# A chunked recurrence with routed experts: the state read on four TensorE tiles, merged copies, and shared PSUM banks

## The chip, the cores and the metric

One core of one Trainium2 chip. The metric is device time in microseconds (us); the kernel before takes 406.6 us (median of three runs).

## What is computed

First an RWKV recurrence over 4 batches, 8 heads, 768 steps and head size 48, then a top-1 routed mixture of 8 experts on its 3072 rows of 384 numbers, all in fp32:

```python
for t in range(S):
    cur = np.einsum('bhd,bhe->bhde', u[None] * kt, vt)
    y[:, :, t] = np.einsum('bhd,bhde->bhe', rt, state + cur)
    state = wt[:, :, :, None] * state + np.einsum('bhd,bhe->bhde', kt, vt)
...
x = y as rows of 8 * 48 numbers
logits = x @ w_gate
e = argmax(logits); gate_w = softmax(logits)[e]
out = gate_w * (maximum(x @ w1[e], 0) @ w2[e])
```

## The kernel before

The sequence is cut into six chunks of 128 steps. A *block* n = 0..23 is one chunk (n // 4) of one batch (n % 4). The 8 heads of a block are kept as 4 pairs q; the two heads j = 0, 1 of a pair lie on partitions 0 to 47 and 64 to 111 of one tile, so that a pair has 112 rows (RP). Where a matmul contracts over one head it uses half of TensorE's rows (0 to 63 or 64 to 127).

For a block, DVE makes the products of the decays in both directions by scans (`suf`, `pre`) and from them `kh` and `rh`. PE multiplies these to the 128x128 attention blocks of all heads (`ap`, `pe_a`). `at` is prepared as a diagonal (the u term, by ACT from `ct`; two of eight by POOL, `pool_diag`), and DVE copies `ap` into it under the causal mask (`dve_at`, L384, two COPY_PREDICATED of 128x512, one for each j). Into `yp` PE first reads the state of the earlier chunks (`pe_inter`, L493, from n = 4 on: 16 trace instructions per block, since each fp32 matmul is two) and then adds `at` times v (`pe_av`, L515). ACT copies `yp` to `yt` (`act_y`); PE transposes it (`yq`), ACT writes it to the rows `xr` (`act_xr`). For the state, `kh` is transposed (`kp`, ACT copies it to `kt`), multiplied with v (`dp`, `pe_state`, L506), and added by DVE to the decayed state (`sst`, `dve_state`); ACT then decays that into `gbd` (`act_g`). The u term is `cp`, ACT's copy `cs`, PE's `cpt`, ACT's copy `ct`.

The order on PE, DVE, ACT and POOL is written by hand: `iteration(n)`, called for n = -3..23, issues the steps of several blocks in turn (`ap`, state read, `at` and `av` of block n; `suf`, `kh`, `pre`, `rh` and `cp` of block n + 2; the diagonal and `kt` of block n + 1; `yq` and `sst` of block n - 1). Each engine works its own list in this order, and waits in it for data or for a buffer.

Routing runs beside the recurrence. When a chunk is done, `logit_mm` (L529, four column tiles of 32, copied by ACT to `ls`) makes the logits of its four blocks; for two chunks at a time (`whole`, at n = 8 and n = 16) `logit_tr` (L540, tile `lpt`) transposes them and `gate` (L544 ff, DVE) finds the expert; one iteration later `rank` and `place` give each row its place in its expert's list, and POOL scatters the rows to DRAM. The last chunks go in smaller lots (n = 21, 22, 23), block 22 by `pe_logits` (L621 ff, eight-column matmuls into `lg`). From n = 22 on the first expert's matmuls (L292) are mixed in; from about 165 us on the experts alone run, their order made by a scheduler; their PE work is the same whatever the recurrence did.

PSUM has eight banks. Before: `psA` one (half of `ap`), `psX` three in turn for all small results (`cp`, `cpt`, `kp`, `yq`, `lp`, `lpt`, `rank`, `lg` and later ones), `psD` one (`dp`), `psY` one (`yp`), `psT` a two-bank tile shared in turn by `pre(n + 2)` and the other half of `ap(n + 1)`: `ap(n + 1)` can start only when `rh(n + 2)` has been read from it.

Of the kernel before, what the change touches and what calls it, by code (L numbers as in the profile page):

```python
# [46 lines left out]

@with_exitstack
def rwkv_moe_kernel(ctx, tc, rkw, vv, ub, wgp, wg, w1, w2, out):
# [247 lines left out]
    def contract(wt, hs, q, rows, t, o=None):  # L297
        op = psX.tile([rows, DM], F32, name="opt", tag="tp")
# [174 lines left out]
    def pe_a(n):  # L473
        if real(n):
            d = blk[n]
            d["ap"] = [psT.tile([P, 2, BANK], F32, name="ap", tag="t")[:, 1, :].rearrange("p (q c) -> p q c", c=C),
                       psA.tile([P, NP_, C], F32, name="ap", tag="ap")]
            for q in range(NP_):
                for j in range(2):
                    rs = slice(64 * j, 64 * j + (64 if j == 0 else D))  # L480
                    nc.tensor.matmul(d["ap"][j][:, q, :], d["kh"][rs, q, :], d["rh"][rs, q, :], start=True, stop=True)  # L481

    def pe_inter(n):
        if real(n):
            d = blk[n]
            yp = psY.tile([RP, NP_, C], F32, name="yp", tag="yp")
            d["yp"] = yp
            if n >= B:
                for q in range(NP_):
# [19 lines left out]
    def pe_av(n):  # L509
        if real(n):  # L510
            d = blk[n]
            for q in range(NP_):
                for j in range(2):
                    h = 2 * q + j
                    nc.tensor.matmul(d["yp"][64 * j:64 * j + D, q, :], d["v"][:, h * D:(h + 1) * D], d["at"][:, j, q, :],  # L515
                                     start=(n < B and q == 0), stop=(q == NP_ - 1), skip_group_check=True)

    def pe_y(n):
        if real(n):
            yq = psX.tile([P, NP_ * P], F32, name="yq", tag="tp")  # L520
# [69 lines left out]
    def rank(k):  # L590
# [635 lines left out]
```

## Time and profile before

| | |
|---|---|
| three timed runs | 406.78, 406.60, 405.75 us |
| profiled execution | 408.01 us, span 406.3 us |
| mean granted TensorE clock | 0.993 |
| PE busy | 386.5 us (95% of the span) |
| DVE busy | 269.8 us (66%) |
| ACT busy | 234.8 us (58%) |
| POOL busy | 117.8 us (29%) |

The table averages two different programs. Up to about 155 us the recurrence keeps three engines busy at once, and an engine's list is read row by row on the timeline, where a bracket gives idle time and what ended it. After that PE works nearly without a gap.

### The profile page before, as it was taken

How to read it: one execution, taken by the hardware profiler on the slowest of the kernel's cores; microseconds unless marked ns; L12 is line 12 of the kernel's file. 1: busy time of each engine (PE TensorE's matmuls, PEld its weight loads, DVE VectorE, ACT ScalarE, POOL GpSimd, SP SyncE). 2: the span in 40 equal slices, each digit the busy share in tenths (PEclk: the TensorE clock that was granted, in tenths of full speed). 3: DMA queues.
4: the chain of work that ended last, by engine and by line, in shares of the span. 5: the costliest groups of instructions: out<-in, count | busy, mean ns of one | idle time of the engine just before them, and what ended most of it. 6: DMA issues, size and time to landing. Idle time of an engine off the chain costs nothing.

```text
span 406.3 us, 9456 instructions
## 1 busy us (share of the span) xinstructions
PE 386.5 (95%) x3537; PEld 347.6 (86%) x3537; DVE 269.8 (66%) x517; ACT 234.8 (58%) x650; POOL 117.8 (29%) x162
## 2 busy tenths in 40 slices
PE   8798999899999889999999999999999999999994
PEld 6566887777777678989888999999999999999993
DVE  8999899999999885726856562472562672632311
ACT  8989898989989873216754543543552562420200
POOL 6552322685417925210300050040040040221001
PEclk9999999999999998999999999999999999999998
DMA  8999999988741223196688447246246253011001
GB/s 209 217 234 227 244 233 240 248 241 212 193 106 60 80 71 118 47 318 199 201 277 234 150 123 229 90 140 214 81 139 215 77 142 132 11 45 37 18 16 41
DMA packets 30158, 62.04 MB, mean 153 GB/s; under 512 B 4879, under 2 KB 17978, under 8 KB 30108
## 3 DMA queue, kind: packets, MB, share of 16 engines
q1 hardware_dynamic: 25500, 51.92, 47.5%
q0 software_dynamic: 4608, 9.48, 7.0%
q8 instruction: 29, 0.48, 0.5%
q14 instruction: 21, 0.17, 0.1%
HBM read 49.53 MB, written 12.20 MB: 152 GB/s over the span
## 4 chain that ended last, share of the span: by engine, by line
PE 71%; DVE 11%; ACT 11%; issue 3%; DMA 2%; POOL 0%; POOLq 0%; SPq 0%; ACTq 0%; DVEq 0%
PE bank L292 26%; PE bank L943 17%; PE opt L304 10%; ACT at L354 3%; DVE pre L376 3%; PE ap L481 2%; DVE suf L360 2%; PE yp L515 2%; PE pt L283 2%; PE yp L493 2%; ACT gbd L413 2%; PE op L932 2%; PE cpt L463 2%; ACT junk L399 2%; PE dp L506 1%
## 5 line engine op out<-in xcount | busy, mean ns | idle before, releaser
L254 POOL DMA_INDIRECT out_dram<-ot,xg x26 | 29.2, 1124 | 169.8 <-DVE ot L933 127.3
L230 DVE TENSOR_TENSOR w2l<-wst,w2h 128x512 fp32r<-128x512 f32 x48 | 31.2, 684 | 43.6 <-ACT w2h L228 43.6
L292 PE MATMUL bank<-xl,w1h 128*128 128x384 f32 (+5 forms) x168 | 59.1, 353 | 0.0
L292 PE MATMUL bank<-xh,w1l 128*128 128x384 f32 (+5 forms) x168 | 58.7, 350 | 0.0
L292 PE MATMUL bank<-xh,w1h 128*128 128x384 f32 (+5 forms) x168 | 53.7, 351 | 0.0
L294 ACT ACTIVATE hh<-bank 128x384 fp32r<-128x384 f32 (+7 forms) x58 | 26.5, 471 | 38.8 <-PE bank L292 37.2
L354 ACT ACTIVATE at<-ident,ct 128x128 f32<-128x128 f32 x144 | 44.6, 392 | 0.1
L295 DVE SCALAR_TENSOR_TENSOR hl<-bank,hh 128x384 fp32r<-128x384 f32 (+7 forms) x58 | 29.9, 531 | 19.7 <-ACT hh L294 18.4
L327 POOL TENSOR_TENSOR rk<-rkwt 112x512 f32<-112x512 f32 x24 | 31.9, 1328 | 33.7 <-DVE pre L364 30.1
L384 DVE COPY_PREDICATED at<-cmask,ap 128x512 f32<-128x512 int32 x48 | 32.5, 729 | 6.4 <-PE ap L481 4.5
L230 DVE TENSOR_TENSOR w1l<-wst,w1h 128x512 fp32r<-128x512 f32 x48 | 31.5, 684 | 6.4 <-ACT w1h L228 6.4
L948 ACT ACTIVATE oT<-bank 128x464 f32<-128x464 f32 (+4 forms) x15 | 7.9, 524 | 46.0 <-PE bank L943 46.0
L228 ACT ACTIVATE w1h<-wst 128x512 fp32r<-128x512 f32 x48 | 28.6, 628 | 9.9 <-PE bank L292 6.7
L943 PE MATMUL bank<-hh,w2l 128*128 128x408 f32 (+4 forms) x96 | 33.9, 355 | 0.0
L943 PE MATMUL bank<-hl,w2h 128*128 128x408 f32 (+4 forms) x96 | 33.8, 354 | 0.0
L943 PE MATMUL bank<-hh,w2h 128*128 128x408 f32 (+4 forms) x96 | 33.5, 354 | 0.0
L676 POOL DMA_INDIRECT xs<-xr,pi x24 | 28.2, 1174 | 16.7 <-DVE sh L550 4.9
L292 PEld LDWEIGHTS bank<-xh,w1l 128*128 128x128 f32 x168 | 31.6, 188 | 0.8
L292 PEld LDWEIGHTS bank<-xl,w1h 128*128 128x128 f32 x168 | 31.5, 188 | 0.8
L481 PE MATMUL ap<-rh,kh 64*128 64x128 f32 (+1 forms) x384 | 27.9, 285 | 4.3 <-DVE rh L337 2.6
L292 PEld LDWEIGHTS bank<-xh,w1h 128*128 128x128 f32 x168 | 31.2, 188 | 0.7
L228 ACT ACTIVATE w2h<-wst 128x512 fp32r<-128x512 f32 x48 | 27.6, 623 | 6.7 <-DMA wst<-in_w_dram 5.9
(169 smaller groups left out, 875.8 us busy)
## 6 DMA issues: line engine op xcount, KB each, us to landing
rkwt<-in_rkw_dram SPq DMA_DIRECT2D x44, 289.5 KB
wst<-in_w_dram SPq DMA_DIRECT2D x48, 256.0 KB
wst<-in_w_dram SPq DMA_DIRECT2D x16, 768.0 KB
vt<-in_vv_dram SPq DMA_DIRECT2D x24, 192.0 KB
xg<-xs SPq DMA_DIRECT2D x6, 579.0 KB
xs<-zrow SPq DMA_DIRECT2D x8, 289.5 KB
rkwt<-in_rkw_dram SPq DMA_DIRECT2D x4, 224.0 KB
xg<-xs SPq DMA_DIRECT2D x1, 675.5 KB
```

The lines of the kernel that those rows point to most:

```text
L228: nc.scalar.activation(hi, st[:, cs], AF.Copy)
L230: nc.vector.tensor_tensor(out=lo, in0=st[:, cs], in1=hi.bitcast(F32), op=ALU.subtract)
L254: i = nc.gpsimd.indirect_dma_start(out=out[:, :], out_offset=bass.IndirectOffsetOnAxis(ap=t.bitcast(I32)[:, q, DM + 1:DM + 2], axis=0), in ...
L292: nc.tensor.matmul(hp, a, x[:, j, :], start=(i == 0), stop=(i == 8))
L295: nc.vector.scalar_tensor_tensor(out=hl, in0=hp, scalar=0.0, in1=hh.bitcast(F32), op0=ALU.max, op1=ALU.subtract)
L304: nc.tensor.matmul(op, a[:, cs], w2v(wt, w, f), start=(i == 0), stop=(i == 23))
L327: i = nc.gpsimd.tensor_tensor(out=d["rk"], in0=d["r"], in1=d["k"], op=ALU.mult)
L354: nc.scalar.activation(blk[n]["at"][:, j, q], ident, AF.Copy, scale=blk[n]["ct"][:, 2 * q + j:2 * q + j + 1])
L384: nc.vector.copy_predicated(out=d["at"][:, j], mask=cmask.unsqueeze(1).broadcast_to([P, NP_, C]), data=d["ap"][j])
L481: nc.tensor.matmul(d["ap"][j][:, q, :], d["kh"][rs, q, :], d["rh"][rs, q, :], start=True, stop=True)
L676: i = nc.gpsimd.indirect_dma_start(out=xsf, out_offset=bass.IndirectOffsetOnAxis(ap=ch["pi", c, b], axis=0), in_=xr[:, b, :], in_offset=No ...
L943: nc.tensor.matmul(pp, w, a, start=(i == 0), stop=(i == 23))
```

## The change

- **Heads swapped in odd pairs.** `head(q, j)` replaces 2q + j. A pair's output halves are swapped where q is odd, so the state read uses (rows 0, columns 0), (rows 64, columns 64), (rows 0, columns 64), (rows 64, columns 0) in turn; before, it used the first two only. `yp` becomes two banks (bank q % 2). The host lays the inputs out to match.
- **`ap` in one two-bank tile**, and the two copies under the mask are one instruction of 128x1024. `sst` goes ahead of it.
- **PSUM.** `kp` goes to `psA`; `cpt`, `lpt` and `rank` of an iteration share one bank (`small(n)`, tile `few`); `psX` has two banks. The experts get five banks from the start and `xbanks` of three.
- **Order.** The diagonal copies on ACT are split, three ahead of `xr` and three behind `kt`. `logit_mm` and `rank` of whole chunks go behind `dp`; `logit_tr` and `gate` of two chunks go behind `av`. At n = 23, `logit_mm` and `logit_tr` replace `pe_logits` for block 22.
- **DMA scratch** of 2048 instead of 4096.

```diff
+def head(q, j):
+    return 2 * q + (j ^ (q & 1))
...
-    psX = mctx.enter_context(tc.tile_pool(name="psX", bufs=3, space=PSUM))
+    psX = mctx.enter_context(tc.tile_pool(name="psX", bufs=2, space=PSUM))
...
+    def small(n):
+        if few.get("n") != n:
+            few["n"] = n
+            few["t"] = xtile([P, BANK], "few")
+        return few["t"]
...
+    def xtile(shape, name):
+        pool, tag = xbanks[nth["x"] % len(xbanks)]
+        nth["x"] += 1
+        return pool.tile(shape, F32, name=name, tag=tag)
...
     def dve_at(n):
...
-            for j in range(2):
-                nc.vector.copy_predicated(out=d["at"][:, j], mask=cmask.unsqueeze(1).broadcast_to([P, NP_, C]), data=d["ap"][j])
+            nc.vector.copy_predicated(out=d["at"].rearrange("p j q c -> p (j q) c"), mask=cmask.unsqueeze(1).broadcast_to([P, 2 * NP_, C]),
+                                      data=d["ap"].rearrange("p j q c -> p (j q) c"))
...
     def pe_coef_tr(n):
...
-            cp = psX.tile([P, H], F32, name="cpt", tag="tp")
+            cp = small(n - 2)[:, 0:H]
...
-            d["kp"] = psX.tile([P, NP_ * RP], F32, name="kp", tag="tp")
+            d["kp"] = psA.tile([P, NP_ * RP], F32, name="kp", tag="ap")
...
     def pe_a(n):
...
-            d["ap"] = [psT.tile([P, 2, BANK], F32, name="ap", tag="t")[:, 1, :].rearrange("p (q c) -> p q c", c=C),
-                       psA.tile([P, NP_, C], F32, name="ap", tag="ap")]
+            d["ap"] = psT.tile([P, 2, BANK], F32, name="ap", tag="t").rearrange("p j (q c) -> p j q c", c=C)
...
     def pe_inter(n):
...
-                        m = 64 if j == 0 else D
-                        rs = slice(64 * j, 64 * j + m)
-                        nc.tensor.matmul(yp[rs, q, :], d["g"][rs, q, 0:m], d["rh"][rs, q, :],
-                                         start=(q == 0), stop=False, skip_group_check=True)
+                        rs = slice(64 * j, 64 * j + (64 if j == 0 else D))
+                        o = 64 * (head(q, j) % 2)
+                        m = 64 if o == 0 else D
+                        nc.tensor.matmul(yp[o:o + m, q % 2, q // 2, :], d["g"][rs, q, 0:m], d["rh"][rs, q, :],
+                                         start=(q < 2), stop=False, skip_group_check=True)
...
     def iteration(n):
...
+        if n == NCH * B - B:
+            xbanks[:] = [(psX, "tp"), (psX, "tp"), (psA, "ap")]
...
         pe_inter(n)
+        dve_state(n - 1)
         dve_at(n)
-        dve_state(n - 1)
...
-        act_diag(n + 1, slice(0, 1) if n < 0 else slice(None))
+        act_diag(n + 1, slice(0, 1) if n < 0 else slice(0, 3))
...
-            pe_logits(n - 1, 1)
+            logit_mm(c, b - 1, 1)
...
+        pe_kt(n + 1)
+        act_kt(n + 1)
+        if n >= 0:
+            act_diag(n + 1, slice(3, None))
+        dve_pre(n + 2)
...
+        pe_state(n)
         if route >= 0 and b == 0:
             logit_mm(route)
         if whole and b == 1:
-            rank(whole)
-        pe_kt(n + 1)
-        act_kt(n + 1)
-        dve_pre(n + 2)
-        if whole and b == 0:
-            logit_tr(whole)
...
-        pe_state(n)
+            rank(whole, n)
         pe_coef_tr(n + 2)
...
-        if whole and b == 0:
-            gate(whole)
...
         pe_av(n)
+        if whole and b == 0:
+            logit_tr(whole, n)
+            gate(whole)
...
-    nc = _bacc.Bacc("TRN2", target_bir_lowering=False, num_devices=1, dynamic_dma_scratch_size=4096)
+    nc = _bacc.Bacc("TRN2", target_bir_lowering=False, num_devices=1, dynamic_dma_scratch_size=2048)
```

The order that comes of it, at three places. **PE, the end of iteration n = 16**, where the logits of two chunks are transposed for the gate (a row is a matmul, or a run of equal ones). Before:

```order
L471 MATMUL kp<-ident,kh 128x112 x4
L540 MATMUL lpt<-ident,ls 128x128 x2
L506 MATMUL dp<-vt,kt 64x48
L506 MATMUL dp<-vt,kt 48x48
L506 MATMUL dp<-vt,kt 64x48
L506 MATMUL dp<-vt,kt 48x48
L506 MATMUL dp<-vt,kt 64x48
L506 MATMUL dp<-vt,kt 48x48
L506 MATMUL dp<-vt,kt 64x48
L506 MATMUL dp<-vt,kt 48x48
L463 MATMUL cpt<-pick,cs 128x8
L515 MATMUL yp<-at,vt 48x128 x8
```

Now (`few` is the bank that holds `cpt`, then `lpt`; the first rows are the last of `lp`):

```order
L548 MATMUL lp<-ytb_199,wgt 32x128
L548 MATMUL lp<-ytb_201,wgt 32x128
L548 MATMUL lp<-ytb_203,wgt 32x128
L548 MATMUL lp<-ytb_195,wgt 32x128
L481 MATMUL few<-pick,cs 128x8
L534 MATMUL yp<-at,vt 48x128 x8
L559 MATMUL few<-ident,ls 128x128 x2
L498 MATMUL ap<-rh,kh 128x128 x8
```

The transposes into `lpt` stood behind `kp`, ahead of `dp` and `av`; they now stand behind `av`, and `lp` behind `dp`.

**PE, the state read of n = 17.** Before:

```order
L481 MATMUL ap<-rh,kh 128x128 x8
L493 MATMUL yp<-rh,gbd_189 64x128
L493 MATMUL yp<-rh,gbd_189 48x128
L493 MATMUL yp<-rh,gbd_189 64x128
L493 MATMUL yp<-rh,gbd_189 48x128
L493 MATMUL yp<-rh,gbd_189 64x128
L493 MATMUL yp<-rh,gbd_189 48x128
L493 MATMUL yp<-rh,gbd_189 64x128
L493 MATMUL yp<-rh,gbd_189 48x128
L522 MATMUL yq<-ident,ytb_197 128x112 x4
```

Now:

```order
L498 MATMUL ap<-rh,kh 128x128 x8
L511 MATMUL yp<-rh,gbd_189 64x128
L511 MATMUL yp<-rh,gbd_189 48x128 x2
L511 MATMUL yp<-rh,gbd_189 64x128 x2
L511 MATMUL yp<-rh,gbd_189 48x128 x2
L511 MATMUL yp<-rh,gbd_189 64x128
L541 MATMUL yq<-ident,ytb_197 128x112 x4
```

Nothing moved but the shapes: before, 64 and 48 columns alternated with the two tiles; now the four matmuls of two pairs go to four tiles.

**DVE, iteration n = 16 and the gate.** Before:

```order
L360 SCALAR_TENSOR_TENSOR suf<-rkwt,sufone 112x520
L364 RECIPROCAL pre_0_175<-suf 112x4
L384 COPY_PREDICATED at<-cmask,ap 128x512 x2
L391 TENSOR_TENSOR sst_194<-dp,gbd_193 112x192
L370 TENSOR_TENSOR kh<-rkwt,suf 112x512
L376 SCALAR_TENSOR_TENSOR pre<-rkwt,pre_0_175 112x520
L337 TENSOR_TENSOR rh<-rkwt,pre 112x512
L548 TENSOR_REDUCE mx<-lpt 128x8
```

Now:

```order
L377 SCALAR_TENSOR_TENSOR suf<-rkwt,sufone 112x520
L381 RECIPROCAL pre_0_175<-suf 112x4
L408 TENSOR_TENSOR sst_194<-dp,gbd_193 112x192
L400 COPY_PREDICATED at<-cmask,ap 128x1024
L387 TENSOR_TENSOR kh<-rkwt,suf 112x512
L393 SCALAR_TENSOR_TENSOR pre<-rkwt,pre_0_175 112x520
L354 TENSOR_TENSOR rh<-rkwt,pre 112x512
L567 TENSOR_REDUCE mx<-few 128x8
```

The two masked copies are one row of 128x1024, `sst` stands ahead of it, and the gate keeps its place in DVE's list, ahead of the next `suf`.

## Rows read from the trace of the kernel before

**Rows 1.** Windows: busy us of PE, PEld, DVE, ACT, POOL; PE clock, DMA share, GB/s
```profile
50.00:100.00 50.00, 47.89 (x745) 38.45 (x742) 48.83 (x85) 45.53 (x156) 24.76 (x31) 1.00 0.95 236
100.00:141.00 41.00, 38.17 (x598) 30.43 (x597) 39.75 (x70) 36.37 (x127) 23.85 (x31) 1.00 0.43 116
...
150.00:160.00 10.00, 9.16 (x103) 7.49 (x100) 7.57 (x37) 3.01 (x10) 5.25 (x10) 0.92 0.22 81
...
170.00:250.00 80.00, 79.00 (x452) 73.00 (x452) 47.39 (x89) 39.06 (x79) 10.82 (x8) 1.00 0.68 204
```

**Rows 2.** Timeline of DVE, n = 16 to the gate (start, us; in brackets idle, releaser)
```profile
109.13 1.23 DVE L360 TENSOR_TENSOR_SCAN suf<-rkwt,sufone 112x520 f32<-112x520 f32 x1
110.39 0.18 DVE L364 RECIPROCAL pre<-suf 112x4 f32<-112x4 f32 x1
110.55 1.36 DVE L384 COPY_PREDICATED at<-cmask,ap 128x512 f32<-128x512 int32 x2
111.82 0.34 DVE L391 TENSOR_TENSOR sst<-dp,gbd 112x192 f32<-112x192 f32 x1
112.08 0.67 DVE L370 TENSOR_TENSOR kh<-rkwt,suf 112x512 f32<-112x512 f32 x1
...
113.94 0.69 DVE L337 TENSOR_TENSOR rh<-rkwt,pre 112x512 f32<-112x512 f32 x1
114.55 0.22 DVE L548 TENSOR_REDUCE mx<-lpt 128x8 f32<-128x64 f32 x1
```

**Rows 3.** Timeline of PE, iteration n = 16
```profile
109.26 1.16 PE L481 MATMUL ap<-rh,kh 64*128 64x128 f32 x16
110.41 1.08 PE L493 MATMUL yp<-rh,gbd 64*64 64x128 f32 x16
111.43 0.60 PE L522 MATMUL yq<-ident,ytb 112*128 112x112 f32 x4
...
112.20 1.06 PE L529 MATMUL lp<-ytb,wgt 112*32 112x128 f32 x32
113.44 0.60 PE L471 MATMUL kp<-ident,kh 112*128 112x112 f32 x4 [0.18 <-ACT xr L431]
113.88 0.38 PE L540 MATMUL lpt<-ident,ls 128*128 128x128 f32 x2
...
115.11 1.08 PE L515 MATMUL yp<-at,vt 128*48 128x128 f32 x16
```

**Rows 4.** Groups of DVE by shape: the copies under the causal mask (busy us, mean ns)
```profile
L384 DVE COPY_PREDICATED at<-cmask,ap 128x512 f32<-128x512 int32 x48 | 32.5, 729 | 6.4 <-PE ap L481 4.5 <-PE yq L522 1.7
```

**Rows 5.** Timeline of DVE: its longest waits in the recurrence, n = 5, 21, 23
```profile
44.19 1.35 DVE L384 COPY_PREDICATED at<-cmask,ap 128x512 f32<-128x512 int32 x2 [1.70 <-PE ap L481]
...
142.21 1.35 DVE L384 COPY_PREDICATED at<-cmask,ap 128x512 f32<-128x512 int32 x2 [1.16 <-PE ap L481]
...
155.29 1.34 DVE L384 COPY_PREDICATED at<-cmask,ap 128x512 f32<-128x512 int32 x2 [1.74 <-PE yq L522]
```

**Rows 6.** Timeline of PE: n = 4, 20, 21, and twice n = 23
```profile
40.45 0.60 PE L471 MATMUL kp<-ident,kh 112*128 112x112 f32 x4 [0.46 <-ACT xr L431]
...
136.40 1.08 PE L493 MATMUL yp<-rh,gbd 64*64 64x128 f32 x16 [0.91 <-ACT ytb L420]
...
144.91 0.39 PE L463 MATMUL cpt<-pick,cs 128*128 128x8 f32 x2 [0.67 <-ACT cs L436]
...
155.35 1.04 PE L627 MATMUL lg<-wgt,ytb 112*128 112x8 f32 x8
...
158.11 1.66 PE L515 MATMUL yp<-at,vt 128*48 128x128 f32 x16
```

**Rows 7.** Windows of 1 us (columns as in rows 1): ahead of the lower clock, and in it
```profile
157.00:158.00 1.00, 0.61 (x5) 0.62 (x5) 0.97 (x4) 0.47 (x1) 0.00 (x0) 1.00 0.53 198
...
159.00:160.00 1.00, 1.00 (x9) 0.64 (x6) 0.83 (x7) 0.18 (x1) 0.95 (x2) 0.50 0.00 0
```

**Rows 8.** Timeline of ACT, iteration n = 16
```profile
114.08 0.55 ACT L449 ACTIVATE kt<-kp 128x448 f32<-128x448 f32 x1 [0.37 <-PE kp L471]
```

More of the change, by code (lines that the diff above doesn't have):

```diff
@@ L280, in transpose_rows @@
         for j in range(3):
-            pt = psX.tile([P, nq * rows], F32, name="pt", tag="tp")
+            pt = xtile([P, nq * rows], "pt")
             for q in range(nq):
@@ L297, in contract @@
     def contract(wt, hs, q, rows, t, o=None):
-        op = psX.tile([rows, DM], F32, name="opt", tag="tp")
+        op = xtile([rows, DM], "opt")
         i = 0
@@ L453, in pe_coef @@
         if real(n):
-            t = psX.tile([P, BANK], F32, name="cp", tag="tp")
+            t = xtile([P, BANK], "cp")
             keep_warm(t[:, C:], 6 if n < 2 else 2 if n < B or n - 3 in (2 * B, 4 * B) else 0)
@@ L513, in pe_av @@
                 for j in range(2):
[L514 to L516 removed]
+                    h = head(q, j)
+                    o = 64 * (h % 2)
+                    nc.tensor.matmul(d["yp"][o:o + D, q % 2, q // 2, :], d["v"][:, h * D:(h + 1) * D], d["at"][:, j, q, :],
+                                     start=(n < B and q < 2), stop=(q >= NP_ - 2), skip_group_check=True)
     def pe_y(n):
         if real(n):
[L520 removed]
+            yq = xtile([P, NP_ * P], "yq")
             for q in range(NP_):
@@ L533, in logit_mm, with logit_tr @@
         ch["ls", c] = ls
-    def logit_tr(k):
+    def logit_tr(k, n):
         c, b, m = k
-        lp = psX.tile([P, m, 32], F32, name="lpt", tag="tp")
+        lp = small(n)[:, H:H + 32 * m].rearrange("p (i e) -> p i e", e=32)
         for i in range(0, m, B):
@@ L593, in rank @@
         oa = ch["old", k]
-        rk = psX.tile([P, GB + 1, E], F32, name="rank", tag="tp")
+        rk = small(n)[:, H + 32 * GB:H + 32 * GB + (GB + 1) * E].rearrange("p (i e) -> p i e", e=E)
         ch["rank", k] = rk
@@ L623, in pe_logits @@
         c, b = divmod(n, B)
-        lg = psX.tile([P, m, E], F32, name="lg", tag="tp")
+        lg = xtile([P, m, E], "lg")
         for i in range(m):
@@ L631, in sort_experts @@
         oa = ch["seen"]
-        cn = psX.tile([P, E], F32, name="cn", tag="tp")
+        cn = xtile([P, E], "cn")
         nc.tensor.matmul(cn, ones, oa, start=True, stop=True)
@@ L656, in check @@
     def check():
-        ng = psX.tile([P, 1], F32, name="ng", tag="tp")
+        ng = xtile([P, 1], "ng")
         nc.tensor.matmul(ng, ones[:RP, :], ch["gb"], start=True, stop=True)
@@ L785, in iteration @@
         if n == NB - 2:
-            rank(lot)
-            logit_mm(c, 2)
+            rank(lot, n)
+            logit_mm(c, 0, 2)
         if n == NB - 1:
-            rank(pair)
+            rank(pair, n)
             act_ex(pair)
@@ L929, in out_tr @@
         def out_tr(j):
-            op = psX.tile([rows, nq, P], F32, name="op", tag="tp")
+            op = xtile([rows, nq, P], "op")
             for q in range(nq):
@@ L986, in rwkv_moe_kernel @@
         pa.mm1(3)
-        rank(end)
+        rank(end, NB + 1)
         place(end)
@@ L1051, in general @@
         nc.vector.tensor_reduce(out=ucol, in_=ubt, axis=AX.X, op=ALU.add)
-        hind = one.tile([RP, 2], F32, name="hind")
+        hind = one.tile([RP, 2, 2], F32, name="hind")
         nc.vector.memset(hind, 0.0)
         for j in range(2):
-            nc.vector.memset(hind[64 * j:64 * j + D, j:j + 1], 1.0)
+            for o in range(2):
+                nc.vector.memset(hind[64 * j:64 * j + D, o, j ^ o:(j ^ o) + 1], 1.0)
         wgt = one.tile([P, 3, E], F32, name="gwg")
@@ L1193, in rows @@
         x = a.reshape(B, NP_, 2, NCH, C, D).transpose(2, 3, 0, 5, 1, 4)
-        t[:, :, 0:D] = x[0]
-        t[:, :, 64:64 + D] = x[1]
+        for q in range(NP_):
+            for j in range(2):
+                t[:, :, 64 * j:64 * j + D, q] = x[head(q, j) % 2, ..., q, :]
         return t
```

57 lines of the change are left out of this document (33 added, 24 removed).

## The prediction

> **What bounds the kernel now.** I read the windows by stage first. In the recurrence DVE is the fullest engine: 48.83 of 50 us, then 39.75 of 41; PE has 47.89 and 38.17, ACT 45.53 and 36.37 [rows 1]. Behind 170 us PE has 79.00 of 80 us and DVE little over half. So up to 141 us a microsecond counts if it is DVE's, and behind 165 if it is PE's; how many of PE's own it can spare in the recurrence is seen on the timelines.
>
> DVE's timeline of n = 16 shows an iteration without a gap: each row starts before the last has quite ended, down to the gate's `mx` at 114.55 [rows 2]. PE's timeline of the same iteration starts `ap(16)` at 109.26 [rows 3], 0.13 us after DVE ended `rh(17)` and began `suf` at 109.13 [rows 2]. That is the shared two-bank tile at work: `ap` waits for `rh`, so PE can't run ahead of DVE, and what PE saves in an iteration only makes it wait longer for the next `rh`. The exceptions are places where DVE waits for PE: 1.70 us at n = 5, 1.16 at n = 21, 1.74 at n = 23 [rows 5]. From n = 20 on DVE has less to do, and the chain through PE and ACT sets the pace: PE waited 0.91 us for ACT's copy of `yp` and 0.67 for `cs` [rows 6]. What arrives earlier at the expert matmuls moves the end by as much, for PE is dense from there.
>
> **The parts and their prices.** The profiled execution took 408.0 us, 1.4 above the median of the three runs, 406.6; the sum is a difference against the profiled one, and I set it against the median.
>
> *Merged copies.* A pair occupies DVE from 110.55 to 111.82, 0.635 us each by start to start [rows 2]; alone one shows 729 ns [rows 4]. What the second start costs isn't shown. From `sst` (192 elements, 0.26 from start to start) and `rh` (512 elements, 0.61) an element costs 0.35 / 320 = 1.09 ns and a start 0.05. The copies at that rate would have 0.635 - 0.56 = 0.08. The bounds are nothing and the whole 0.18 of a 4-element RECIPROCAL [rows 2]. I take 0.07, near the rows of like size: 21 copies up to n = 20 give **-1.5**, three in the tail **-0.2**; with the bounds 0 and -4.3 in all. Not below nothing, since no element is added.
>
> [...]
>
> *State read.* It takes 111.43 - 110.41 = 1.02 us for 16 instructions, 64 ns each, on two tiles [rows 3]. The logits `lp`, on four column tiles, take 1.06 us for 32, 33 ns each, with as many columns moved in each. Four tiles for the state read then give 16 x 33 = 0.53 plus a tail: 0.45 saved, between 0 (no more in parallel) and 0.49. Twenty blocks have it, 9 us of PE, but nearly all goes into a longer wait for `rh`. It counts at n = 4 (within the next item), and in the chain behind n = 20.
>
> *The wait of n = 5.* `at(5)` waited 1.70 us for `ap(5)`. In the iteration ahead of it PE loses 0.46 at `kp`, waiting for ACT's `xr` to free a bank [rows 6]; `kp` now has a bank of its own and `xr` comes three diagonal copies earlier. With 0.45 of the state read, `ap(5)` comes 0.9 earlier, and `sst` (0.26) is done inside the rest of the wait instead of behind it: **-1.1**. Bounds: -0.3 (`sst` alone) and -1.7. Of the 4.5 us that the masked copies wait for `ap` [rows 4], 2.9 are the first two of rows 5; of the other 1.6, small waits of some tenths, I take a third to go: **-0.5**, between 0 and -1.6.
>
> *The gate behind `av`.* At n = 16 `lpt` began at 113.88 and took 0.38, so it was there before DVE came to the gate at 114.55 [rows 2, 3]. Now all of PE's iteration precedes it. From 109.26, by starts and lengths of the rows: `ap` 1.15, the read 1.02 - 0.45, `yq` and `cp` 0.77, `lp` 1.06, `kp` 0.44, `dp`, `cpt` and `lpt` 115.11 - 113.88 = 1.23, `av` 1.08: 115.6 [rows 3]. DVE is there at about 114.45, and has nothing else in its list: 1.15 us lost, at n = 8 and at n = 16, **+2.3**. Behind the gate stand `suf` and all of DVE's next iteration; `rh`, `ap` and POOL's product follow. Bounds: 0.5 each (PE slack that I miss) and 1.6 (a state read of 1.02).
>
> Up to n = 20 this makes -1.5 - 1.1 - 0.5 + 2.3 = **-0.8**.
>
> *The tail.* From n = 20 PE's `cp` to `cpt` wait (0.67) and its wait for `y` (0.91) [rows 6] shrink, since `cs` comes ahead of three diagonal copies, and the state read is 0.45 shorter. By carrying the starts forward by hand `ap(21)` comes 1.4 earlier and `ap(23)` 1.7, of which 0.8 was counted: **-0.9**, bounds 0 and -1.8. The state read of 23 then stands straight ahead of the expert work: **-0.45**. At n = 23 the eight-column logits (1.04 us in 8 instructions [rows 6]) become four 128-column matmuls on one column tile and a transpose: **+0.2**, bounds -0.4 and +0.5.
>
> *Costed at nothing.* The rank moved behind `dp` (it has an iteration until `place`); the split diagonal copies (they are needed five microseconds later; what stands behind them is `ct`, which waited for `cpt` anyway); `psX` of two (by the order `yq`, `cp`, shared bank, each bank is read two steps before it comes round; where that cover goes, it costs the 0.18 to 0.46 that a wait for `xr` costs now [rows 3, 6]); the two output banks for ACT's copy of `yp`; the smaller scratch, whose scatters move the same bytes. SP's and POOL's orders don't change.
>
> Sum: -0.8 - 0.2 - 0.9 - 0.45 + 0.2 = **-2.15**: 405.85 against the profiled 408.0, **404.5** against the median.
>
> **The rivals.**
>
> [...]
>
> *No change.* The copies give nothing (+1.7) or the tail gives nothing (+0.9), while the gates cost what they show: 405.5 to 407. This holds too if the state read doesn't go faster: +0.45 at n = 4, in the tail and at n = 23, 405.9. [...]
>
> *Slower.* ACT has 45.53 of 50 us [rows 1], and at n = 16 waited 0.37 for `kp` [rows 8]. Before, six diagonal copies filled the time until `yq` and `cp` were there; now ACT comes to `xr`, `cs` and `kt` 0.9 us earlier and may wait at each, with three copies still to do behind. If the state read is not shorter and this adds 0.3 to ACT's iteration, ACT takes over from DVE, which has under 0.03 of slack in a microsecond: 16 iterations with `kt` lose up to 4.8, the copies' gain is hidden, and the tail's remains: 406.6 + 4.8 - 1.3 = 410.1; with half of it 407.8. It decides from the point where ACT's waits at `xr`, `cs` and `kt` together exceed the 0.37 that it waits now, in most iterations. Against it: what it waits ahead of `kt` it need not wait behind it, at `ct`.
>
> *The change doesn't do what it says* only for the copies, if the chip handled 1024 elements as two; that is the lower bound above.
>
> **How the numbers follow.** 0.3% (1.2 us) is what a measurement here tells from no change. The forecast, 404.5, has 0.42 (its own range 403.4 to 405.4); with the clock kept up, 0.20; no change, 405.4 to 407.8, 0.22; slower, 0.16. Faster is 0.62. The range takes in the case of the clock with the copies at half their upper bound (402.9 - 2), and the upper end of no change: 401.0 to 407.7. Out of it are most of the slower case and a little below.
>
> **What would show it.** Right: state-read rows of about 0.6 us; one masked copy of about 1.25; a bracket of about 1.2 at `mx` at n = 8 and 16, released by PE; about 1 us less at `at(5)`; the first expert matmul 2 us earlier. Wrong: ACT with longer waits at `xr` or `kt` than it had at `ct`; a state read of 1.02; a copy of 1.36; `mx` without a wait; a change behind 170 us, where I count none.

## The result, and the profile after

The changed kernel took 410.32 us (median of six runs, 408.14 to 416.55), the kernel before 405.5 on the same occasions (405.08 to 406.78). The ratio is 1.0106, 95% interval 1.0058 to 1.0154: slower by 1%, where the forecast was faster by 0.5%. Ratios, here and below, are of the fast executions alone, so this one leaves out the 416.55; medians are of all executions. The profiled execution took 411.14 us, span 409.4, at a mean granted TensorE clock of 0.973; before it was 408.01, span 406.3, at 0.993.

The windows by stage, which answer to [rows 1] (the same columns):

```profile
50.00:100.00 50.00, 47.06 (x700) 36.51 (x699) 44.34 (x72) 41.97 (x143) 21.93 (x29) 0.86 0.92 238
100.00:141.00 41.00, 36.68 (x582) 28.75 (x580) 38.29 (x64) 37.01 (x127) 20.61 (x27) 0.96 0.52 131
...
160.00:170.00 10.00, 9.30 (x76) 8.79 (x76) 6.01 (x30) 2.88 (x9) 3.80 (x8) 0.83 0.24 87
170.00:250.00 80.00, 78.87 (x464) 72.68 (x464) 49.20 (x106) 39.56 (x81) 11.90 (x10) 1.00 0.66 197
```
The time behind 170 us is the same: 78.87 of 80 us of PE. What was lost lies in the recurrence, between 50 and 100 us: DVE, the engine that bounds it, is busy 44.34 us instead of 48.83, and the granted clock, 1.00 there before, has a mean of 0.86. Where, DVE's list tells. The table has the start of `pre(n + 2)`, issued once in each iteration n, from the two timelines:

| n | before | after | difference |
|---|---|---|---|
| -2 | 5.61 | 5.92 | +0.31 |
| 0 | 16.62 | 18.02 | +1.40 |
| 4 | 39.17 | 39.68 | +0.51 |
| 5 | 46.29 | 46.86 | +0.57 |
| 8 | 62.67 | 62.74 | +0.07 |
| 9 | 70.77 | 72.22 | +1.45 |
| 10 | 77.33 | 78.83 | +1.50 |
| 11 | 83.39 | 87.81 | +4.42 |
| 16 | 112.67 | 116.61 | +3.94 |
| 17 | 120.58 | 125.75 | +5.17 |
| 19 | 132.10 | 137.47 | +5.37 |
| 21 | 144.04 | 147.98 | +3.94 |

So 1.1 us are lost at the start and won back by n = 8; 1.4 go between n = 8 and 9, 2.9 between 10 and 11, 1.2 between 16 and 17; from n = 19 to 21 1.4 are won. Of the 3.9 us at n = 21, 3.1 are left at the end of the span (409.4 against 406.3). DVE's timeline at these places (gate of n = 8, the masked copy of n = 9, that of n = 11, gate of n = 16):

```profile
66.06 0.23 DVE L567 TENSOR_REDUCE mx<-few 128x8 f32<-128x64 f32 x1 [1.35 <-PE few L559]
...
68.50 0.18 DVE L381 RECIPROCAL pre<-suf 112x4 f32<-112x4 f32 x1
68.60 0.33 DVE L408 TENSOR_TENSOR sst<-dp,gbd 112x192 f32<-112x192 f32 x1
68.85 1.32 DVE L400 COPY_PREDICATED at<-cmask,ap 128x1024 f32<-128x1024 int32 x1
70.05 0.68 DVE L248 TENSOR_TENSOR w1l<-wst,w1h 128x512 fp32r<-128x512 f32 x1
...
85.42 1.30 DVE L400 COPY_PREDICATED at<-cmask,ap 128x1024 f32<-128x1024 int32 x1 [3.01 <-PE ap L498]
...
120.10 0.23 DVE L567 TENSOR_REDUCE mx<-few 128x8 f32<-128x64 f32 x1 [1.53 <-PE few L559]
```
The gate waits 1.35 and 1.53 us for the transposed logits (`few`), where it had begun without a gap before [rows 2]. The merged copy occupies 68.85 to 70.05, 1.20 us, where the pair took 1.27 [rows 2]; from the reciprocal to the end of copies and `sst` it is 1.55, against 1.69 (110.39 to 112.08). Then, at n = 11, DVE waits 3.01 us for `ap`. PE's timeline tells why:

```profile
60.56 0.67 PE L511 MATMUL yp<-rh,gbd 64*64 64x128 f32 x16
61.16 0.60 PE L541 MATMUL yq<-ident,ytb 112*128 112x112 f32 x4
...
70.97 1.08 PE L534 MATMUL yp<-at,vt 128*48 128x128 f32 x16
74.24 2.08 PE L498 MATMUL ap<-rh,kh 64*128 64x128 f32 x16 [2.19 <-DVE rh L354]
76.24 1.13 PE L511 MATMUL yp<-rh,gbd 64*64 64x128 f32 x16
77.30 1.01 PE L541 MATMUL yq<-ident,ytb 112*128 112x112 f32 x4
...
127.77 1.95 PE L498 MATMUL ap<-rh,kh 64*128 64x128 f32 x16 [1.95 <-DVE rh L354]
```
The state read starts 0.60 us ahead of `yq`, against 1.02 [rows 3]: the four tiles do work side by side. Behind `av` of n = 9 PE then has nothing to do for 2.19 us, because `rh` is late: it had kept on working while DVE stood at the gate, and DVE's list of n = 9 is a long one. When `rh` comes, `ap` takes 2.0 us from start to start instead of 1.1, the state read 1.06 instead of 0.60, `yq` 0.94 instead of 0.53. Windows of 1 us at this place (columns as in [rows 1], the clock is the third number from the end) show the cause:

```profile
72.00:73.00 1.00, 0.05 (x2) 0.00 (x0) 1.00 (x2) 1.00 (x4) 0.00 (x0) 1.00 1.08 172
73.00:74.00 1.00, 0.00 (x0) 0.00 (x0) 0.96 (x2) 1.00 (x6) 0.38 (x1) 0.67 1.00 224
74.00:75.00 1.00, 0.76 (x6) 0.77 (x8) 0.93 (x5) 0.89 (x4) 0.03 (x1) 0.50 1.12 342
...
86.00:87.00 1.00, 1.00 (x12) 0.66 (x4) 1.00 (x2) 0.00 (x0) 0.06 (x1) 0.50 0.90 159
87.00:88.00 1.00, 1.00 (x14) 0.55 (x12) 1.00 (x3) 0.67 (x2) 0.00 (x0) 1.00 0.98 296
```
In the microsecond in which PE does nothing the granted clock falls from 1.00 to 0.50, and it stays there for 13 us. PE is busy all of every microsecond from 75 us to the end of it, and DVE waits 3.01 us for `ap`: here, at the lower clock, PE and not DVE bounds the recurrence. The same comes behind the second gate: 1.95 us idle ahead of `ap` at 127.77, and about 4 us at 0.50. The fall that the kernel before had at 158 [rows 7] is there too, at 165.

### The profile page after: what moved, and what is told of

Read it like the earlier page. It is cut to its first block, busy times and chain, and to the rows that moved or that the text cites. A ratio compares the mean times of both kernels' runs of the same rounds, so it can differ in the third digit from the quotient of the medians.

```text
span 409.4 us, 9409 instructions
## 1 busy us (share of the span) xinstructions
PE 385.9 (94%) x3538; PEld 344.6 (84%) x3538; DVE 269.1 (66%) x493; ACT 234.7 (57%) x651; POOL 117.8 (29%) x162
## 4 chain that ended last, share of the span: by engine, by line
PE 64%; DMA 16%; DVE 11%; issue 2%; SPq 2%; ACT 2%; POOL 0%; POOLq 0%; DVEq 0%; ACTq 0%
PE bank L309 23%; PE bank L967 17%; PE opt L321 8%; DMA vt<-in_vv_dram 7%; DMA rkwt<-in_rkw_dram 4%; PE ap L498 3%; DMA wst<-in_w_dram 3%; DVE pre L393 2%; DVE at L400 2%; DMA xs<-zrow 2%; PE pt L300 2%; PE yp L534 2%; PE op L956 2%; PE yp L511 2%; PE yq L541 1%
## 5 line engine op out<-in xcount | busy, mean ns | idle before, releaser
L272 POOL DMA_INDIRECT out_dram<-ot,xg x26 | 30.1, 1158 | 169.1 <-DVE ot L957 126.6
L371 ACT ACTIVATE at<-ident,ct 128x128 f32<-128x128 f32 x144 | 47.1, 397 | 0.1
L498 PE MATMUL ap<-rh,kh 64*128 64x128 f32 (+1 forms) x384 | 30.9, 303 | 10.3 <-DVE rh L354 8.7
L498 PEld LDWEIGHTS ap<-rh,kh 64*128 64x128 f32 (+1 forms) x384 | 25.8, 203 | 15.8 <-DVE rh L354 11.3
L400 DVE COPY_PREDICATED at<-cmask,ap 128x1024 f32<-128x1024 int32 x24 | 31.6, 1316 | 6.2 <-PE ap L498 6.1
```

What stands on the lines that cost most here:

```text
L272: i = nc.gpsimd.indirect_dma_start(out=out[:, :], out_offset=bass.IndirectOffsetOnAxis(ap=t.bitcast(I32)[:, q, DM + 1:DM + 2], axis=0), in ...
L400: nc.vector.copy_predicated(out=d["at"].rearrange("p j q c -> p (j q) c"), mask=cmask.unsqueeze(1).broadcast_to([P, 2 * NP_, C]), data=d[" ...
L498: nc.tensor.matmul(d["ap"][:, j, q, :], d["kh"][rs, q, :], d["rh"][rs, q, :], start=True, stop=True)
```

## The experiments

The chips differ by up to 3 us in the kernel before, so each kernel is compared with the kernel before on its own chip; medians of different rows below are not to be set against each other where the middle column differs by more than a few tenths.

| run | median us | before, same chip | ratio | 95% interval |
|---|---|---|---|---|
| e1_gate_early | 405.39 | 405.0 | 0.9998 | 0.9981 to 1.0015 |
| e2_gate_late | 409.45 | 405.0 | 1.0143 | 1.0064 to 1.0222 |
| e3_two_tiles | 409.24 | 405.0 | 1.0110 | 1.0072 to 1.0148 |
| e5_warm | 405.67 | 405.0 | 1.0020 | 0.9998 to 1.0041 |
| e6_gate_next | 404.26 | 405.38 | 0.9978 | 0.9951 to 1.0005 |
| e7_scratch | 411.27 | 405.38 | 1.0157 | 1.0119 to 1.0196 |
| e8_own_bank | 404.29 | 405.38 | 0.9971 | 0.9954 to 0.9987 |
| e9_gate_next_cold | 406.7 | 405.38 | 0.9997 | 0.9959 to 1.0034 |
| e10_mixed | 407.77 | 407.88 | 0.9991 | 0.9955 to 1.0026 |
| e11_own_two_copies | 408.37 | 407.88 | 1.0003 | 0.9970 to 1.0037 |
| e12_own_two_tiles | 408.91 | 407.88 | 1.0027 | 0.9996 to 1.0057 |
| e13_mixed_warm | 402.64 | 405.14 | 0.9929 | 0.9905 to 0.9953 |

**Is it the gate?** First the routing order of before in the changed kernel, and the other way round the moved gate alone in the kernel before.

`e1_gate_early`:

```diff
+        if route >= 0 and b == 0:
+            logit_mm(route)
+        if whole and b == 1:
+            rank(whole, n)
         pe_kt(n + 1)
...
+        if whole and b == 0:
+            logit_tr(whole, n)
         pe_state(n)
-        if route >= 0 and b == 0:
-            logit_mm(route)
-        if whole and b == 1:
-            rank(whole, n)
...
+        if whole and b == 0:
+            gate(whole)
...
         pe_av(n)
-        if whole and b == 0:
-            logit_tr(whole, n)
-            gate(whole)
```

> The changed kernel with the routing steps of whole chunks in the old order (logits behind cp, their transposes ahead of dp, the gate behind rh without a wait). Theory (the gate's wait): DVE's waits of 1.35 and 1.53 us at the gate go, PE's idle 2.19 and 1.95 us ahead of the next-but-one ap go with them, and the clock stays at 1.00 between 70 and 135 us: 2.9 (clock) + 2.6 (gates) less than the changed kernel's profiled run, about 403 to 404, faster than before. Rival (the shorter state read leaves PE too idle): the clock falls at some other place in the recurrence and the time stays above 406. Rival (smaller DMA scratch slows loads): DVE still loses the 1.1 us of the start, and the time is 405 or more.

Measured: as fast as before, 0.9998, and no fall of the clock between 70 and 140 us in its profile. The 1% is undone. The expected gain didn't come, and the gate still waits, as DVE's timeline shows:

```profile
66.37 0.23 DVE L567 TENSOR_REDUCE mx<-few 128x8 f32<-128x64 f32 x1 [0.81 <-ACT ct L460]
...
116.75 0.23 DVE L567 TENSOR_REDUCE mx<-few 128x8 f32<-128x64 f32 x1 [1.34 <-ACT ct L460]
```
The order alone doesn't free it: `lpt` now lies in one tile and bank with `cpt`, which PE writes behind `dp`, and DVE is let go only when ACT has read `cpt` (`ct` in the brackets; 0.81 and 1.34 us). `e8_own_bank` tests this below.

`e2_gate_late`, in the kernel before:

```diff
-        if route >= 0 and b == 0:
-            logit_mm(route)
-        if whole and b == 1:
-            rank(whole)
         pe_kt(n + 1)
...
-        if whole and b == 0:
-            logit_tr(whole)
...
         pe_state(n)
+        if route >= 0 and b == 0:
+            logit_mm(route)
+        if whole and b == 1:
+            rank(whole)
...
-        if whole and b == 0:
-            gate(whole)
...
         pe_av(n)
+        if whole and b == 0:
+            logit_tr(whole)
+            gate(whole)
```

> The kernel before with only this moved: logits and rank of whole chunks behind dp, their transposes and the gate behind av. State read, copies, banks and scratch as before. Theory (the gate's wait): DVE waits 1.5 to 1.8 us at each gate (PE's iteration is 0.4 longer here than in the changed kernel), PE then idles over 1 us ahead of ap(10) and ap(18), the clock falls in some executions; 408 to 411 us. Rival (the shorter state read is what lets the clock fall): two waits of about 1.6 and no fall, 408 at most.

Measured: 1.0143 (1.0064 to 1.0222, four executions). Moving the gate is enough to make the kernel before slower, by about as much as the whole change does. DVE's timeline has the two waits and, as its last row, the masked copy of n = 21, which the account of the prediction comes back to; PE's has the idle stretch behind the first wait:

```profile
67.39 0.23 DVE L548 TENSOR_REDUCE mx<-lpt 128x8 f32<-128x64 f32 x1 [1.57 <-PE lpt L540]
...
119.65 0.23 DVE L548 TENSOR_REDUCE mx<-lpt 128x8 f32<-128x64 f32 x1 [1.63 <-PE lpt L540]
...
145.74 1.34 DVE L384 COPY_PREDICATED at<-cmask,ap 128x512 f32<-128x512 int32 x2
```
```profile
75.64 1.84 PE L481 MATMUL ap<-rh,kh 64*128 64x128 f32 x16 [1.58 <-DVE rh L337]
```
The clock fell there for about 4 us in this execution. The shorter state read isn't needed for that. But the fall cost little: `pre` is later than in the kernel before by 1.66 from n = 8 to 9 and by 1.43 from n = 16 to 17, which are the two waits, and by only 0.28 from n = 10 to 11; another of the four executions took 409.57 us at a mean clock of 0.999. What this run loses is mostly the waits themselves, and 1.12 at the start.

**Is it the state read, or the scratch?** `e3_two_tiles` is the changed kernel with `head(q, j) = 2 * q + j`, so that the read is on two tiles again.

> The changed kernel with the heads of odd pairs unswapped: the state read is on two tiles again (about 1.02 instead of 0.60), all else as changed. Theory (the gate's wait): the wait at the gate grows by about 0.4 at n = 8 and 16, PE still idles before ap(10) and ap(18), the clock still falls: 409 to 413. Rival (the shorter read makes PE idle and the clock fall): no fall in the recurrence, 405 to 407.

Measured: 409.24, 1.0110, the same as the change. The profiled execution, the longest of the seven (413.53), has a fall of the clock at 77 to 83 us; the gates wait 1.93 and 2.37 us. The rival by which the clock falls only because the read is shorter is out. `e7_scratch` is the changed kernel with the scratch of 4096:

> The changed kernel with the DMA scratch of 4096 as before, nothing else. Theory (gate and clock): no difference from the changed kernel, 408 to 413, with the clock falling as there. Rival (the smaller scratch delays loads at the start, 1.1 us, or elsewhere): 1 us or more less, and DVE's start as in the kernel before.

Measured: 411.27, 1.0157, with falls at 72 and at 123 us. The larger scratch makes it no faster; the interval (1.0119 to 1.0196) overlaps that of the change. Its profile happens to have none of the loss at the start, though: `pre` starts 0.09 earlier than before at n = 0 (after: 1.40 later) and 2.39 earlier at n = 8. That loss isn't the scratch's: `e2_gate_late`, with 4096 too, starts n = 0 1.12 later, and `e3_two_tiles`, with 2048, only 0.39.

**Wait and clock apart.** `e5_warm` leaves the gate's wait and fills PE's idle stretch with matmuls that nothing uses:

```diff
         pe_av(n)
+        if whole and b == 1:
+            keep_warm(blk[n + 2]["cw"], 9)
```

> The changed kernel with nine idle matmuls of 384 bf16 columns (about 0.21 us each) behind av of n = 9 and n = 17, in the place where PE idles 2.19 and 1.95 us. They compute nothing that is used. The DVE's wait at the gate stays. Theory: the clock stays at 1.00 up to 140 us, the gates still cost 1.35 and 1.53: some 3 us less than the changed kernel, 406 to 407. If the idle stretch is not what lets the clock fall, it falls as in the changed kernel and the time stays at 410.

Measured: 405.67, 1.0020. PE's timeline and 1-us windows at the first place:

```profile
74.82 1.64 PE L143 MATMUL cp<-wz,ones 128*128 128x384 bf16 x9
77.34 1.16 PE L499 MATMUL ap<-rh,kh 64*128 64x128 f32 x16 [0.88 <-DVE rh L354]
```
```profile
75.00:76.00 1.00, 1.00 (x8) 0.61 (x7) 1.00 (x2) 1.00 (x3) 0.00 (x0) 1.00 1.09 226
76.00:77.00 1.00, 0.46 (x3) 0.07 (x1) 0.97 (x2) 1.00 (x5) 0.28 (x1) 1.00 1.02 248
```
The nine matmuls leave 0.88 us of the 2.19 idle, and the clock stays at 1.00 from 70 to 100 and from 120 to 140 us. Against the 1% of the change, 0.2% is left, and the two intervals don't overlap: idle matmuls alone are worth some 3.5 us here by the two ratios, more than the gate's two waits. (In this execution the clock fell at 46 us instead, behind a pause of PE inside `ap(5)`; see the last section.)

`e6_gate_next` takes the wait away as well, by moving the gate behind `suf` of the next iteration in DVE's list; `e9_gate_next_cold` is the same without the nine matmuls:

```diff
+            gate(whole)
             act_ex(whole)
...
             logit_tr(whole, n)
-            gate(whole)
```

> The changed kernel with the gate of two chunks moved on in DVE's list, behind suf of the next iteration (its transposes stay behind av), and the nine idle matmuls of the run before it behind av of n = 9 and 17. Theory: neither gate waits (its data is there 1 us before DVE comes to it), PE has no idle stretch over 1 us there, the clock stays at 1.00: 2.9 us less than e5_warm (405.67), about 403, faster than both kernels. Rival (the experts' weights set the end, by their DMA): the recurrence ends about 2.9 earlier than in e5_warm, but PE waits for weights between 190 and 215 us and the time stays at 404.3 or more.

> e6_gate_next without the idle matmuls. Neither gate waits, but PE still comes to ap(10) and ap(18) about 2 us ahead of rh. Theory (PE's idle stretch lets the clock fall): the clock falls there in some executions, 404 to 408 and widely spread. If the waiting gate itself were the cause, 403 and no fall.

Measured: 0.9978 with the matmuls, 0.9997 without, on one chip, with intervals that overlap: the times don't tell the two apart, nor either from the kernel before. The executions without the matmuls lie between 403.1 and 410.1, but for one of 2008.74; those with them between 402.3 and 408.2. In neither profile does the gate wait more than 0.16 us. So the clock can fall without a waiting gate, behind PE's idle stretch in the iteration that follows, as PE's timeline and windows of the cold one show at n = 17:

```profile
120.66 1.89 PE L498 MATMUL ap<-rh,kh 64*128 64x128 f32 x16 [1.14 <-DVE rh L354]
```
```profile
119.00:120.00 1.00, 0.52 (x10) 0.26 (x6) 0.97 (x2) 1.00 (x3) 0.00 (x0) 1.00 0.00 0
120.00:121.00 1.00, 0.34 (x4) 0.34 (x6) 0.96 (x3) 1.00 (x5) 0.41 (x1) 0.95 0.36 89
121.00:122.00 1.00, 1.00 (x14) 1.00 (x12) 0.97 (x2) 1.00 (x6) 0.00 (x0) 0.50 0.30 108
```
This fall cost DVE nothing (`pre` is 1.94 earlier than before at n = 17, 2.03 at n = 18). At 71.68 the same execution had an idle stretch of 1.43 us and no fall: whether one of over a microsecond is followed by a fall differs from place to place and from run to run. The changed kernel's wide spread goes with the clock: its mean falls from 0.983 in the execution of 408.63 us to 0.951 in that of 416.55.

**The shared bank.** `e8_own_bank` is `e1_gate_early` with

```diff
-        lp = small(n)[:, H:H + 32 * m].rearrange("p (i e) -> p i e", e=32)
+        lp = (small(n)[:, H:H + 32 * m] if m != 2 * B else xtile([P, 32 * m], "lpt")).rearrange("p (i e) -> p i e", e=32)
```

> e1_gate_early with the transposed logits of two chunks in a bank of psX of their own instead of the one shared with cpt. Theory (the gate waited 0.81 and 1.34 us in e1_gate_early because it shares a bank with cpt, which PE writes behind dp): both waits fall under 0.3 us, and the time is 1.5 to 2 us less than e1_gate_early (405.39), 403.5. If the wait is for lpt itself, which is late since lp waits for xr (0.24 and 0.59), the waits stay at 0.5 or more. Rival (the weights' DMA sets the end): 404.3 or more whatever the waits.

Measured: 404.29, 0.9971 (0.9954 to 0.9987): faster than both kernels. DVE's timeline at the gate of n = 8:

```profile
64.57 0.69 DVE L354 TENSOR_TENSOR rh<-rkwt,pre 112x512 f32<-112x512 f32 x1
65.18 0.22 DVE L567 TENSOR_REDUCE mx<-lpt 128x8 f32<-128x64 f32 x1
```
The gate begins 0.61 us behind the start of `rh`, without a wait. So it had been the sharing with `cpt`; as the logits get a tile of their own as well as a bank, the run doesn't tell which of the two held the gate. The gain is less than what the two waits were, and two rows of PE's timeline tell of it:

```profile
40.23 1.08 PE L548 MATMUL lp<-ytb,wgt 112*32 112x128 f32 x32 [0.87 <-ACT xr L449]
...
205.84 0.29 PE L300 MATMUL pt<-ident,xg 108*128 108x108 f32 x1 [1.35 <-DMA xg<-xs]
```
With two banks in `psX` the early `lp` waits for `xr` (0.87 at n = 4, ahead of `ap(5)`), and PE waits 1.35 us for the rows of an expert, a transfer: in this execution, what the recurrence wins is partly given back there. PE's timeline of the kernel before shows no such wait.

**What the parts are worth.** Three kernels on a chip where the kernel before took 407.88 and had a mean clock of 0.965 to 0.973 in five of 30 executions; their intervals overlap, so only the profiles tell something.

`e10_mixed`: as `e8_own_bank`, but the early place of `logit_mm` only `if whole and b == 0`, and the rank behind `dp` as in the change.

> e8_own_bank with the logits of a chunk early only where a gate follows in the same iteration (n = 8 and 16); those of n = 4, 12 and 20, and the two ranks, stay behind dp as in the change. Theory: lp no longer waits for xr at n = 4 (0.87 us in e8_own_bank) ahead of ap(5), at(5) comes some 0.8 us earlier, the rank no longer waits 0.41 for the gate at n = 17; the gates still don't wait. 0.5 to 1 us less than e8_own_bank (404.29): 403.5. If DVE is ahead there anyway or the experts' loads set the end: as e8_own_bank.

Measured: 0.9991, and the executions spread from 404.64 to 415.28; inconclusive as a time. In the profile `pre` of n = 20 starts 1.13 earlier than in `e8_own_bank`, 0.52 of it won at n = 5; its clock then fell at 142, behind a wait of 1.81 us of PE for ACT's `cs`.

`e11_own_two_copies`: `e8_own_bank` with the masked copies apart. `e12_own_two_tiles`: `e8_own_bank` with the state read on two tiles.

> e8_own_bank with the masked copies as two instructions of 128x512 again. By the rows (1.20 from start to start for the merged one, 1.25 to 1.27 for two) 0.06 a block: up to 1.4 us more than e8_own_bank, 405.0 to 405.7, DVE later by 0.06 a block. [...]

> e8_own_bank with the state read on two tiles (heads unswapped). Theory (the read is hidden behind rh in the recurrence and counts only where PE is late): 0.3 to 1.3 us more than e8_own_bank, mainly at n = 5, 13, 17 and behind n = 20: 404.6 to 405.6. If the read's 0.42 counted in each of 20 blocks: 8 more. If the shorter read were what lets the clock fall: less than e8_own_bank, and less spread.

Measured: 1.0003 and 1.0027. Neither is clearly slower than before, and the times can't price a part of a microsecond. In the profile of the first two copies take 1.24 to 1.25 us from start to start, against 1.21 for the merged one in `e8_own_bank`: 0.03 to 0.04 a block, and DVE takes 0.38 longer from n = 5 to n = 20. That of the second shows where the state read counts:

```profile
97.73 1.16 PE L498 MATMUL ap<-rh,kh 64*128 64x128 f32 x16
99.24 1.08 PE L511 MATMUL yp<-rh,gbd 64*64 64x128 f32 x16 [0.35 <-ACT ytb L438]
```
With the read at 1.02 PE doesn't wait for `rh` at this place, but for ACT's copy of `yp` (0.35 us), and is itself late. From n = 8 to n = 20 DVE wins 1.34 us against before in `e8_own_bank` and loses 0.57 in this one, so the shorter read is worth some 1.9 us there, by these profiles (0.52 of it a wait of the gate of n = 16 for `lpt`).

**A version that beats both.** `e13_mixed_warm` is `e10_mixed` with three idle matmuls where PE waits for `rh`:

```diff
         pe_av(n)
+        if n in (9, 10, 11, 13, 14, 17, 18):
+            keep_warm(blk[n + 2]["cw"], 3)
```

> e10_mixed with three idle matmuls of 384 bf16 columns (0.63 us) behind av of n = 9, 10, 11, 13, 14, 17 and 18, where PE waits 0.55 to 0.86 us for rh in e10_mixed. They compute nothing that is used. Theory (PE's waits are what lets the clock fall, and filling them costs nothing): no fall between 70 and 140 us, DVE not later than in e10_mixed, the executions closer together than those of e10_mixed (404.64 to 415.28), faster than the kernel before by 1.5 to 2 us. If the idle matmuls push av's successors: DVE later by some tenths at each of the seven places, as slow as before or slower.

Measured: 402.64 against 405.14, 0.9929 (0.9905 to 0.9953), and the six executions lie within 401.69 to 403.76. PE's timeline at n = 10 and the two windows of the recurrence:

```profile
77.15 0.66 PE L143 MATMUL cp<-wz,ones 128*128 128x384 bf16 x3
78.30 1.16 PE L499 MATMUL ap<-rh,kh 64*128 64x128 f32 x16 [0.49 <-DVE rh L354]
```
```profile
50.00:100.00 50.00, 48.34 (x778) 36.70 (x776) 49.14 (x79) 46.70 (x160) 25.97 (x32) 1.00 1.01 256
100.00:141.00 41.00, 38.57 (x629) 29.49 (x631) 39.88 (x63) 38.77 (x137) 24.24 (x33) 1.00 0.41 114
```
DVE is as full as in the kernel before, 49.14 and 39.88 us [rows 1], and gets through more of its list in them; the clock is 1.00 in both windows. How much of this the idle matmuls give isn't shown: `e10_mixed` ran on another chip, its `pre` wins as much on the kernel before from n = 0 to n = 20 (3.13 us, here 3.26), and its fall of the clock, at 142 us, lies where this kernel fills nothing.

## Why the prediction was wrong

**The step that failed** is the one on the gate behind `av`. Its wait was foreseen and about rightly priced: 1.15 us each, measured 1.35 and 1.53 (+0.6 together). But the step followed only DVE: "1.15 us lost". It didn't ask what PE does when DVE is behind, and so the sum has TensorE's clock in the recurrence at nothing. PE runs on through the wait, stands still for 2.19 us one iteration later, and the clock falls from 1.00 to 0.50: 2.9 us between n = 10 and 11, and a few tenths behind the second gate. The prediction gave the clock a part only in the case of its being kept up where it fell at 158 us [rows 7], and as a gain; that a change which shortens PE's list and stalls DVE makes new falls wasn't among the cases. `e5_warm` shows it: with the waits left as they are and the idle stretch filled, the ratio goes from 1.0106 to 1.0020, some 3.5 us. `e1_gate_early` agrees: its gates still wait 0.81 and 1.34 us, the clock doesn't fall there, and it is as fast as before. The 402.9 in the prediction's range is 404.5 less 1.6 us for the clock kept up at 158; no run shows that term: in the changed kernel's profile the fall is there too and as long, from 165 to 169, and in `e13_mixed_warm`, where the clock is 1.00 from 140 to 170 us, this gain can't be told from the others.

**The slower rival** had the right sign by another mechanism: ACT taking over. It didn't in `e13_mixed_warm`, which has the split diagonal too and a clock of 1.00 in both windows of the recurrence: ACT's waits at `xr`, `cs` and `kt` between 20 and 140 us sum to 4.5 us, where the kernel before waited 2.5 at `kt` and 6.7 at `ct`, and DVE stays the fullest engine.

**The other terms**, by the same profile:
- Merged copies: forecast 0.07 a block, measured 0.03 to 0.04 (`e11_own_two_copies`). The whole stretch with `sst` is 0.14 shorter, so some 0.1 comes from `sst` going ahead, which the prediction counted only at n = 5.
- State read: 0.60 measured, 0.57 forecast: on four tiles, two to each half of the rows, the read is 0.42 shorter than on two.
- Where the state read counts: the prediction had nearly all of the saving go into a longer wait for `rh`, and counted it at n = 4 and behind n = 20 only. That was wrong too, the other way: from n = 5 to 8 `pre` gains 0.17 a block on the kernel before in `e8_own_bank`, and nothing in `e3_two_tiles` and `e12_own_two_tiles`, where the read takes 1.02. In the kernel before PE's rows follow one another there without a gap, 5.45 us a block, as on PE's timeline:

```profile
48.36 1.16 PE L481 MATMUL ap<-rh,kh 64*128 64x128 f32 x16
...
53.81 1.16 PE L481 MATMUL ap<-rh,kh 64*128 64x128 f32 x16
```
So PE set the pace of these blocks as much as DVE did. The prediction read the start of `ap(16)`, 0.13 us behind the end of `rh`, as a wait; its row has no idle time in a bracket either [rows 3].
- The wait of n = 5: -1.1 forecast, nothing won in this execution (+0.51 to +0.57). `av(4)` came 0.2 earlier, but `ap(5)` was broken off by a pause (below). In `e7_scratch`, without the pause, DVE wins 0.92 at this place.
- The small waits: -0.5 forecast. One is seen: at n = 4 the kernel before waits 0.44 us for `ap`, the changed one doesn't, and all eleven runs made from the changed kernel win 0.54 to 0.58 from n = 3 to 4, where `e2_gate_late` wins nothing.
- The tail: -0.9 and -0.2 forecast from n = 19 to 21, -1.4 measured. The size is about right, but it isn't shown to be the change's: `e2_gate_late`, whose tail is that of the kernel before, wins 1.27 there too. Its masked copy of n = 21 starts without a wait (row above), where the kernel before waited 1.16 [rows 5]; with DVE later, PE and ACT are not.
- Unforeseen: +1.1 at n = 0, which also `e2_gate_late` has (+1.12) and `e7_scratch` hasn't (-0.09), so it isn't the change's (most of it is explained in the last section).

With the gates at 2.9, no gain at n = 5, the start and the clock, the sum of -2.15 becomes -2.15 + 0.6 + 1.1 + 1.4 + 3.2 = +4.2, where the two profiled executions differ by 3.1. The rest isn't settled term by term: the copies gave half of what they were counted for, and the state read, by `e8_own_bank` against `e12_own_two_tiles`, more.

## What to carry to other kernels

When a change makes one engine wait, follow the others through the wait: one that runs on will stand still later, and if that is TensorE, it can lose its clock: in the recurrence here it fell behind idle stretches of 1.14 to 2.44 us, for 4 to 14 us, and not behind others of 1.37 to 1.54. A long fall cost more than the wait itself: 2.9 us behind a gate's wait of 1.35. Slack that becomes idle time in one piece can be worth filling with matmuls that compute nothing: some 3.5 us in `e5_warm`. And results that share a tile and its PSUM bank can share their waits: with the logits beside `cpt`, DVE's gate hung on a later matmul and its reader, whatever the order said, for 0.81 and 1.34 us in `e1_gate_early`.

## What the runs showed that wasn't expected

A lower clock is not equally dear everywhere. The fall at 73 us cost 2.9 us, that at 128 us, shorter, about 0.3: while it lasted DVE, late by the gate, was busy 0.97 of each microsecond or more, and was the bound for most of it. The other profiles agree. By the starts of `pre` against the kernel before, the falls of about 4 us (`e2_gate_late`, `e7_scratch` at 72, `e9_gate_next_cold`) cost 0 to 0.3, those of about 7 (`e3_two_tiles`, `e5_warm`) 1.6 and 2.6, the one of about 13 (`e7_scratch` at 123) 3.6. What sets the length of a fall is not known from these runs.

PE paused inside `ap(5)`, in a run of matmuls that wait for nothing that the profile shows:

```profile
42.71 0.48 PE L498 MATMUL ap<-rh,kh 64*128 64x128 f32 x3
43.89 1.04 PE L498 MATMUL ap<-rh,kh 48*128 48x128 f32 x13 [0.69 <-issue]
```
The pause was 0.69 us here, 1.44 in `e5_warm` (where the clock fell behind it), 0.26 to 0.97 in five other runs, and none is listed in the rest. Its cause wasn't tried.

In the start, `kh` took 1.66 us where 0.73 was usual, while POOL's product `rk` ran beside it (POOL's and DVE's timelines):

```profile
16.28 1.27 POOL L344 TENSOR_TENSOR rk<-rkwt 112x512 f32<-112x512 f32 x1 [2.27 <-DMA rkwt<-in_rkw_dram]
```
```profile
16.45 1.66 DVE L387 TENSOR_TENSOR kh<-rkwt,suf 112x512 f32<-112x512 f32 x1
```
`rk` was let go by a late load, so it ran beside `kh` instead of beside the masked copies, which the traces show at 1.30 to 1.37 us, beside it or not. The runs, though not made for it, show what happens. In all twelve traces where `rk` starts first, `kh` ends 0.54 to 0.56 us behind the end of `rk`, whether it lasts 0.67, 0.88, 1.24 or 1.78 us: as long as `rk` runs, `kh` hardly gets on. In the two where `kh` starts first, by 0.01 and 0.03 us (`e11_own_two_copies`, `e3_two_tiles`), `kh` takes 0.68 and it is `rk` that takes longer, 1.80 and 1.78 instead of 1.27. Of the 1.1 us lost at the start, 0.93 is the longer `kh`, and that depends on when `rk` is let go; the hand-made dependency that holds `rk` back to the copies is in the kernel before already.
